# A list scheduler inside the kernel orders the work of every engine: cross attention with a state, then a mixture-of-depths layer

## The chip, the cores and the metric

The kernel runs on one core of a Trainium2 chip. Its engines, TensorE (PE), VectorE (DVE), ScalarE (ACT), GpSimd (POOL) and SyncE (SP), each carry out a queue of instructions in order and wait for each other by semaphores. The metric is the device time of one execution in microseconds; the median of three runs of the kernel before is 334.57 us (334.52 to 334.78).

## The reference

Inputs: x of 8 batches, 8 heads, 512 rows of 64; a state of 32 rows per batch and head; a gate vector of 512; weights w1 (512 x 1024) and w2 (1024 x 512). All is float32, and 128 rows of each batch are chosen.

```python
scores = scale * x @ state.T                 # per batch and head
a = exp(scores - max); a /= sum(a) + 1e-9
xread = a @ state                            # 512 rows
a2 = softmax over x of scale * state @ x.T   # the other direction
sread = a2 @ x                               # 32 rows
x2 = concat([xread, sread], rows), heads side by side   # 8 x 544 x 512
s = x2 @ w_gate                              # one score per row
for b in range(8):
    top = the 128 rows of batch b with the largest s
    out[b] = x2[b]
    out[b, top] += sigmoid(s[top]) * (relu(x2[b, top] @ w1) @ w2)
```

## The kernel before, in words

The work on a batch falls into three parts. The **attention** turns x on TensorE (`turn_x`, L181, copies on ScalarE, L183), multiplies it with the turned state (`scores`, L193), and runs two softmaxes on the same scores: one over the state, for which VectorE transposes blocks of 32 into a tile `e` and back into `eT` (`soft_a` and `soft_b`, L203 to L229), and one over x, on the scores as they lie (`a`, L212). `reads` makes the x read from `eT` (L245, copied by L246 into `xs`) and the state read from the turned `a` (L255, L265, scaled into `xt` by L267). The **choice** multiplies `xs` and `xt` with the gate (`gate_scores`, L291, L295, L298, L299), turns the scores into a row (`score_row`, L306 to L310), compares each with all later ones (`later_wins`, L320), counts the wins on TensorE (L340), makes a one-hot matrix of places (L350) and picks the rows' numbers with a matmul (`gather`, L361); GpSimd then fetches the 128 rows from the output in memory, where `store_base` has put the batch. The **network** (`mlp`) turns the fetched rows (L397), does the first layer (L406, eight groups of columns with a relu on ScalarE, L408) and the second (L415), adds the gated result to the rows (L419) and GpSimd writes them back (L420). It is done for the groups of batches [0], [1], [2, 3], [4, 5], [6, 7].

The order of every engine is that of the code. A loop goes over the batches; at four places of a batch `fill(3.4)` draws pieces of the network from a Python generator that yields an estimate (3.5 us a piece) until 3.4 us are filled. A piece of the first layer is 16 matmuls, one of the second 4. PSUM has two banks with the tag `tr` for all transposes and small products, two banks `h` for the network, and one double bank each for the scores (`s`) and the x read (`o`).

The function that the diff touches is the whole program:

Of the kernel before, what the change touches and what calls it, by code (L numbers as in the profile page):

```python
# [18 lines left out]
def kernel(  # L19
# [38 lines left out]
    N_X, N_XR = 5, 6  # L58
    const = pool("const", 1)
    xin = pool("xin", N_X)  # L60
    work = pool("work", 2)
    xrow = pool("xrow", 2)
    small = pool("small", 4)
    psum = pool("psum", 2, space=bass.MemoryType.PSUM)

    def bank(tag):
        return psum.tile([128, 512], F32, name=f"ps_{tag}", tag=tag)

    def banks(tag):
        return psum.tile([128, 1024], F32, name=f"ps_{tag}", tag=tag, bufs=1)  # L70


    ctx.enter_context(tc.manual_schedule(engines={ENG.PE, ENG.DVE, ENG.Activation, ENG.SP}))
# [3 lines left out]
    xf = {}  # L77

    def load_x(b, pieces=2):
        xf[b] = xin.tile([128, H, NC, D], F32, name="xf")  # L80
        n = H // pieces
        for h in range(0, H, n):
            nc.sync.dma_start(out=xf[b][:, h:h + n], in_=x[b, h:h + n].rearrange("h (p c) d -> p h c d", c=NC))


    st_c = xin.tile([128, B, 2, 2, D], F32, name="st_c", tag="xf")
    st_src = state.rearrange("b (g q) n d -> (q n) b g d", g=2)
    for u in range(2):
        nc.sync.dma_start(out=st_c[:, 0, :, u], in_=st_src[:, 0])
    load_x(0, 4)  # L90
    nc.sync.dma_start(out=st_c[:, 1:B, :, 0], in_=st_src[:, 1:B])

    wg = const.tile([128, Dm], F32, name="wg")
    nc.sync.dma_start(out=wg, in_=bass.AP(tensor=moe_w_gate.tensor, offset=moe_w_gate.offset,
                                          ap=[[0, 128], [1, Dm]]))
    load_x(1)
    load_x(2)
    w1 = const.tile([128, ND, F], F32, name="w1")
    w2 = const.tile([128, NF, Dm], F32, name="w2")
    nc.sync.dma_start(out=w1, in_=moe_w1.rearrange("(j p) f -> p j f", p=128))  # L100
    load_x(3)
    nc.sync.dma_start(out=w2, in_=moe_w2.rearrange("(j p) m -> p j m", p=128))

    ident = const.tile([128, 128], F32, name="ident")
    make_identity(nc, ident)
    z0 = small.tile([128, 1], F32, name="z0")
    nc.vector.memset(z0, 0.0)
    nc.scalar.activation(out=z0, in_=z0, func=AF.Exp)


    st_v = const.tile([128, B, 2, 2 * D], F32, name="st_v")

    def state_V(lo, hi):
# [5 lines left out]
    nc.gpsimd.memset(st_v[:, 0:1], 0.0)  # L119
    state_V(0, 1)  # L120
    nc.gpsimd.tensor_copy(out=st_c[:, 1:B, :, 1], in_=st_c[:, 1:B, :, 0])
    nc.gpsimd.memset(st_v[:, 1:B], 0.0)
    state_V(1, B)

    wg_s = const.tile([128, 2, D], F32, name="wg_s")
    for q in range(4):
        nc.gpsimd.tensor_copy(out=wg_s[Ns * q:Ns * (q + 1)],
                              in_=wg[Ns * q:Ns * (q + 1)].rearrange("p (g m) -> p g m", g=2)[:, :, D * q:D * (q + 1)])


    after = const.tile([128, SP], F32, name="after")
    nc.gpsimd.iota(after, pattern=[[1, SP]], base=0, channel_multiplier=-1, allow_small_or_imprecise_dtypes=True)
    nc.gpsimd.tensor_scalar(after, after, 0.0, None, op0=ALU.is_gt)

    places = const.tile([128, NC + 1, n_slots], F32, name="places")
    nc.gpsimd.iota(places, pattern=[[-128, NC + 1], [1, n_slots]], base=0, channel_multiplier=-1,
                   allow_small_or_imprecise_dtypes=True)
    ones = const.tile([128, 1], BF16, name="ones")
    nc.gpsimd.memset(ones, 1.0)

    same_n = const.tile([128, Ns], F32, name="same_n")

    sc = const.tile([128, B, NC + 1], F32, name="sc")
    nc.gpsimd.memset(sc, 0.0)
    aux = const.tile([128, B, NC + 1, 5], BF16, name="aux")
    num = const.tile([128, 2, B, NC + 1], I32, name="num")
    nc.gpsimd.iota(num[:, 0, :, 0:NC], pattern=[[SP, B], [1, NC]], base=0, channel_multiplier=NC)
    nc.gpsimd.iota(num[:, 0, :, NC], pattern=[[SP, B]], base=S, channel_multiplier=1)  # L150
# [9 lines left out]
    st_T = const.tile([128, B, 2, 128], F32, name="st_T")  # L160

    def state_T(lo, hi):
        for b in range(lo, hi, 2):
            n = min(2, hi - b)
            ps = bank("tr").rearrange("p (b g m) -> p b g m", b=2, g=2)
            for bb in range(n):
                for g in range(2):
                    nc.tensor.transpose(ps[:, bb, g], st_c[:, b + bb, g].rearrange("p u d -> p (u d)"), ident)  # L168
            nc.scalar.activation(out=st_T[:, b:b + n], in_=ps[:, 0:n], func=AF.Copy, scale=scale)  # L169


    xT = {}

    def turn_x(b):

        xT[b] = []
        for h in range(0, H, 2):
            ps = bank("tr").rearrange("p (k r t) -> p k r t", k=2, r=2)
            for k in range(2):
                for r in range(2):  # L180
                    nc.tensor.transpose(ps[:, k, r], xf[b][:, h + k, 2 * r:2 * r + 2].rearrange("p w d -> p (w d)"), ident)  # L181
            t = work.tile([128, 2, 2, 128], F32, name="xT", tag="xT", bufs=6)
            nc.scalar.copy(out=t, in_=ps)  # L183
            xT[b].append(t)

    def scores(b):

        ps = banks("s").rearrange("p (w g t) -> p w g t", w=2, g=2)
        for g in range(2):
            for q in range(4):  # L190
                for w in range(2):
                    half = slice(D * w, D * (w + 1))
                    nc.tensor.matmul(ps[Ns * q:Ns * (q + 1), w, g], st_T[half, b, g, Ns * q:Ns * (q + 1)],  # L193
                                     xT[b][2 * g + q // 2][half, q % 2].rearrange("p r t -> p (r t)"),
                                     start=True, stop=True)
        del xT[b]
        return ps

    def soft_a(ps):

        e = work.tile([128, 32, Ns], F32, name="e")
        flat = e.rearrange("p j n -> p (j n)")
        nc.vector.transpose(out=flat, in_=ps.rearrange("p w g t -> p (w g t)"))  # L203
        nm = small.tile([128, 2], F32, name="nm")
        nc.vector.tensor_reduce(out=nm, in_=ps.rearrange("p w g t -> p g w t"), axis=AX.XY, op=ALU.max, negate=True)  # L205
        mx = small.tile([128, 32], F32, name="mx")
        nc.vector.reduce_max(out=mx, in_=e, axis=AX.X)  # L207
        nc.vector.tensor_tensor(out=e, in0=e, in1=mx.to_broadcast([128, 32, Ns]), op=ALU.subtract)  # L208
        a = work.tile([128, 2, 2, 256], F32, name="a", tag="a", bufs=1)
        ss = small.tile([128, 2], F32, name="ss")  # L210
        for g in range(2):
            nc.scalar.activation(out=a[:, g], in_=ps[:, :, g], func=AF.Exp, bias=nm[:, g:g + 1],  # L212
                                 accum_out=ss[:, g:g + 1])
        nc.scalar.activation(out=flat, in_=flat, func=AF.Exp)
        return e, a, ss

    def soft_b(e, a, ss):

        flat = e.rearrange("p j n -> p (j n)")
        sm = small.tile([128, 32], F32, name="sm")  # L220
        nc.vector.reduce_sum(out=sm, in_=e, axis=AX.X)
        nc.vector.tensor_scalar_add(sm, sm, 1e-9)
        nc.vector.reciprocal(out=sm, in_=sm)
        nc.vector.tensor_tensor(out=e, in0=e, in1=sm.to_broadcast([128, 32, Ns]), op=ALU.mult)
        eT = work.tile([128, 2, 2, 2, 128], F32, name="eT")
        nc.vector.transpose(out=eT.rearrange("p w g r t -> p (w g r t)"), in_=flat)
        rs = small.tile([128, 2], F32, name="rs")
        nc.vector.tensor_scalar_add(rs, ss, 1e-9)  # L228
        nc.vector.reciprocal(out=rs, in_=rs)  # L229
        return eT, a, rs  # L230

    xs, xt = {}, {}

    def reads(b, eT, a, rs):

        xs[b] = xrow.tile([128, NC, Dm], F32, name="xs")
        xt[b] = xrow.tile([128, 2, D], F32, name="xt")

        def x_read(r):
# [232 lines left out]
    for i in range(1, B + 1):  # L472
# [4 lines left out]
        if i < B:  # L477
            ps = scores(i)
# [63 lines left out]
```

## Time and profile before

| | |
|---|---|
| median of three runs | 334.57 us |
| the profiled execution | 335.67 us |
| its span, first to last instruction | 333.9 us |
| mean granted TensorE clock | 0.815 |
| TensorE busy | 239.7 us (72%) |
| VectorE busy | 147.8 us (44%) |
| ScalarE busy | 84.9 us (25%) |

The span is one execution as the hardware profiler saw it. Busy is the time in which an engine had an instruction under way. The granted clock is the share of full speed (2.4 GHz) that TensorE was given; a single stretch is at full or at half speed, or a mean of both.

### The profile page before, as it was taken

How to read it: one execution, taken by the hardware profiler on the slowest of the kernel's cores; microseconds unless marked ns; L12 is line 12 of the kernel's file. 1: busy time of each engine (PE TensorE's matmuls, PEld its weight loads, DVE VectorE, ACT ScalarE, POOL GpSimd, SP SyncE). 2: the span in 40 equal slices, each digit the busy share in tenths (PEclk: the TensorE clock that was granted, in tenths of full speed). 3: DMA queues.
4: the chain of work that ended last, by engine and by line, in shares of the span. 5: the costliest groups of instructions: out<-in, count | busy, mean ns of one | idle time of the engine just before them, and what ended most of it. 6: DMA issues, size and time to landing. Idle time of an engine off the chain costs nothing.

```text
span 333.9 us, 4768 instructions
## 1 busy us (share of the span) xinstructions
PE 239.7 (72%) x1928; PEld 166.1 (50%) x1928; DVE 147.8 (44%) x430; ACT 84.9 (25%) x159; POOL 28.9 (9%) x44
## 2 busy tenths in 40 slices
PE   4308532939992999449597998894949995949993
PEld 3106421738651865237375853453637742428741
DVE  0065639182638182685138537842097315510010
ACT  4027160333313313143115323231131400011100
POOL 4820000100011001100100010011000011010011
PEclk9957855778997898956587979598597976978999
DMA  7995420260054004500300040004000120010000
GB/s 196 315 384 214 171 90 1 84 208 3 0 172 152 2 0 151 174 0 34 133 2 0 0 167 2 32 29 171 0 0 2 69 99 31 1 63 2 0 31 31
DMA packets 17559, 26.86 MB, mean 80 GB/s; under 512 B 5632, under 2 KB 13824, under 8 KB 16512
## 3 DMA queue, kind: packets, MB, share of 16 engines
q1 hardware_dynamic: 16256, 22.35, 19.5%
q0 software_dynamic: 1280, 4.20, 3.9%
q8 instruction: 15, 0.25, 0.3%
q14 instruction: 8, 0.07, 0.1%
HBM read 15.53 MB, written 11.01 MB: 79 GB/s over the span
## 4 chain that ended last, share of the span: by engine, by line
PE 58%; DVE 21%; ACT 7%; DMA 5%; issue 5%; POOL 3%; SPq 1%; POOLq 0%; DVEq 0%; ACTq 0%
PE ps_h L406 19%; PE ps_h L415 17%; PE ps_o L245 6%; DVE scr L291 3%; DMA xr<-out_dram,idx 3%; PE ps_tr L181 3%; DVE e L203 3%; DVE mx L207 3%; DVE nm L205 3%; DVE e L208 3%; PE ps_tr L265 2%; PE ps_s L193 2%; PE ps_tr L361 2%; ACT xs L246 2%; DMA st_c<-in_state_dram 2%
## 5 line engine op out<-in xcount | busy, mean ns | idle before, releaser
L406 PE MATMUL ps_h<-xg,w 128*128 128x256 f32 (+1 forms) x320 | 72.5, 394 | 14.3 <-ACT xg L398 14.3
L406 PEld LDWEIGHTS ps_h<-xg,w 128*128 128x128 f32 x320 | 60.9, 229 | 24.2 <-ACT xg L398 16.0
L415 PE MATMUL ps_h<-w,hT 128*128 128x512 f32 x128 | 68.4, 691 | 0.0
L415 PEld LDWEIGHTS ps_h<-w,hT 128*128 128x128 f32 x128 | 27.2, 220 | 31.9 <-issue 31.6
L181 PE MATMUL ps_tr<-ident,xf 128*128 128x128 f32 x128 | 22.8, 335 | 16.6 <-ACT xT L183 15.9
L181 PEld LDWEIGHTS ps_tr<-ident,xf 128*128 128x128 f32 x128 | 17.9, 170 | 21.4 <-ACT xT L183 18.4
L212 ACT ACTIVATE a<-ps_s,nm 128x512 f32<-128x512 f32 x16 | 10.8, 682 | 61.0 <-DVE nm L205 61.0
L320 DVE SCALAR_TENSOR_TENSOR win<-srow,sc,after 128x544 bf16<-128x544 f32 (+4 forms) x40 | 18.1, 513 | 18.3 <-ACT srow L310 18.3
L367 POOL DMA_INDIRECT xr<-out_dram,idx x8 | 8.0, 994 | 208.6 <-DVE z L373 169.2
L408 ACT ACTIVATE hT<-ps_h 128x512 f32<-128x512 f32 x16 | 9.5, 595 | 63.5 <-PE ps_h L406 63.5
L246 ACT COPY xs<-ps_o 128x1024 f32<-128x1024 f32 x16 | 16.2, 1013 | 33.2 <-PE ps_o L245 33.2
L203 DVE STREAM_TRANSPOSE e<-ps_s 128x1024 f32<-128x1024 f32 x8 | 10.0, 1246 | 33.1 <-PE ps_s L193 31.4
L245 PE MATMUL ps_o<-st_v,eT 64*128 64x128 f32 x256 | 21.6, 317 | 3.5 <-DVE rs L228 2.9
L245 PEld LDWEIGHTS ps_o<-st_v,eT 64*128 64x128 f32 x256 | 18.4, 218 | 8.8 <-DVE rs L228 3.0
L291 DVE SCALAR_TENSOR_TENSOR scr<-xs,wg 128x512 f32<-128x512 f32 x32 | 22.1, 690 | 1.3
L183 ACT COPY xT<-ps_tr 128x512 f32<-128x512 f32 x32 | 17.8, 585 | 7.0 <-PE ps_tr L181 6.7
L267 DVE TENSOR_TENSOR xt<-ps_tr,rs 128x128 f32<-128x128 f32 x8 | 2.3, 292 | 35.8 <-PE ps_tr L265 35.8
L419 DVE SCALAR_TENSOR_TENSOR ot<-ps_h,z,xr 128x512 f32<-128x512 f32 x8 | 6.0, 750 | 26.7 <-PE ps_h L415 26.5
L168 PE MATMUL ps_tr<-ident,st_c 128*128 128x128 f32 x16 | 3.3, 356 | 18.5 <-ACT st_T L169 14.3
L420 POOL DMA_INDIRECT out_dram<-ot,idx x8 | 8.3, 1036 | 86.9 <-DVE ot L419 42.6
L397 PE MATMUL ps_tr<-ident,xr 128*128 128x128 f32 x32 | 7.0, 358 | 11.0 <-DMA xr<-out_dram,idx 11.0
L361 PE MATMUL ps_tr<-aux,oh 128*128 128x5 bf16 (+1 forms) x40 | 7.2, 180 | 10.0 <-DVE oh L350 9.4
(80 smaller groups left out, 238.2 us busy)
## 6 DMA issues: line engine op xcount, KB each, us to landing
out_dram<-xs SPq DMA_DIRECT2D x8, 1024.0 KB, 4.0
xf<-in_x_dram SPq DMA_DIRECT2D x14, 512.0 KB, 6.9
w<-in_moe_w_dram SPq DMA_DIRECT2D x2, 2048.0 KB
xf<-in_x_dram SPq DMA_DIRECT2D x4, 256.0 KB
out_dram<-xt SPq DMA_DIRECT2D x32, 16.0 KB, 3.1
st_c<-in_state_dram SPq DMA_DIRECT2D x1, 448.0 KB
wg<-in_moe_w_gate_dram SPq DMA_DIRECT2D x1, 256.0 KB
st_c<-in_state_dram SPq DMA_DIRECT2D x2, 64.0 KB, 1.9
```

What stands on the lines that cost most here:

```text
L181: nc.tensor.transpose(ps[:, k, r], xf[b][:, h + k, 2 * r:2 * r + 2].rearrange("p w d -> p (w d)"), ident)
L183: nc.scalar.copy(out=t, in_=ps)
L203: nc.vector.transpose(out=flat, in_=ps.rearrange("p w g t -> p (w g t)"))
L205: nc.vector.tensor_reduce(out=nm, in_=ps.rearrange("p w g t -> p g w t"), axis=AX.XY, op=ALU.max, negate=True)
L212: nc.scalar.activation(out=a[:, g], in_=ps[:, :, g], func=AF.Exp, bias=nm[:, g:g + 1], accum_out=ss[:, g:g + 1])
L245: nc.tensor.matmul(po[:, i, w, g], eT[half, w, g, r], st_v[half, b, g], start=True, stop=True)
L246: nc.scalar.copy(out=xs[b][:, 2 * r:2 * r + 2].rearrange("p w (g i m) -> p w g i m", g=2, i=2), in_=po.rearrange("p i w g m -> p w g i m"))
L291: nc.vector.scalar_tensor_tensor(scr, xs[b][:, c], 1.0, wg, op0=ALU.mult, op1=ALU.mult, accum_out=sc[:, b, c:c + 1])
L320: nc.vector.scalar_tensor_tensor(w[0:n], srow[0:n, f:SP], sc[0:n, b, c:c + 1], after[0:n, 0:SP - f], op0=ALU.is_gt, op1=ALU.mult, accum_ou ...
L361: nc.tensor.matmul(pa[0:m, 0:5], oh[0:n, c, lo:hi], aux[0:n, b, c], start=(c == 0), stop=(c == NC))
L406: nc.tensor.matmul(ph[:, f, 0:n], w1[:, j, 128 * (f0 + f):128 * (f0 + f + 1)], xg[:, j], start=(j == 0), stop=(j == ND - 1))
L415: nc.tensor.matmul(py[0:m], hT[:, f, lo:lo + m], w2[:, f], start=(f == 0), stop=(f == NF - 1))
```

## The change

The program no longer issues its instructions where the code stands. It describes pieces: each has an engine, a length in us that was written down, the pieces that it comes after, the buffers that it takes from a ring or uses, and a key. A scheduler, `carry_out`, then issues them: it keeps a clock for each engine, finds for each piece that can go the time at which its engine, its predecessors (0.2 us later if on another engine) and its buffers are free, takes the engine with the earliest such piece, and issues on it the piece of the smallest key among those that can start within 0.25 us of it. Keys are (batch, step) for attention and choice and (100 + group, step) for the network, so the network comes where nothing else can start; its copies and final products come first wherever they are ready. GpSimd's queue is ordered so too.

With it change: the groups of batches of the network, the size of its pieces (4 or 8 matmuls in the first layer, 2 in the second), the buffers of fetched rows (8 instead of 6), and rings of some other small tiles. Behind each indirect DMA GpSimd sets one small tile to zero. The split of the row numbers (`row_numbers`) becomes a piece with a late key. What is computed, and by which instructions, stays the same.

```diff
-    N_X, N_XR = 5, 6
+    N_X, N_XR = 5, 8
...
+    def carry_out():
+        free = {}
+        left = list(pieces)
+        HOP, SOON = 0.2, 0.25
+        while left:
+            ready = []
+            for p in left:
+                if any(q.end is None for q in p.after) or any(buf.ap is None for buf in p.uses):
+                    continue
+                at = max([free.get(p.engine, 0.0)] + [(q.end + HOP if q.engine != p.engine else q.done) for q in p.after])
...
+            t, e = min(((at, p.engine) for at, p in ready), key=lambda r: r[0])
+            at, p = min(((at, p) for at, p in ready if p.engine == e and at <= t + SOON), key=lambda r: r[1].key)
+            for buf in p.takes:
+                buf.ring.take(buf)
+            p.fn()
+            free[e] = p.done = at + p.length
+            p.end = p.done + p.lands
...
+    p_num = add("DVE", 1.0, row_numbers, after=[p_tab], key=(0, 40))
...
+        p = add("DVE", 1.25, turn_in, after=[p_s], takes=[e], uses=[s], key=key(2))
+        p = add("DVE", 1.2, x_max, after=[p], uses=[e], key=key(2))
...
+            p = add("PE", 1.16, read, after=[p_eT, p_pool], takes=[o], uses=[eT], key=key(5))
...
+        return [add("SP", 3.0, x_rows, after=p_xs, uses=[xs], key=(b, 7), lands=1.5),
+                add("SP", 0.4, s_rows, after=[p_xt], key=(b, 7), lands=2.5)]
+    def by_number(b, **kw):
+        touches(b, nc.gpsimd.indirect_dma_start(**kw), True)
+        nc.gpsimd.memset(z1, 0.0)
...
+            for f in range(nf):
+                p = add("PE", 1.86 if nf == 2 else 1.0, lambda f0=f0, f=f, go=first_layer: go(f0, f), after=p_xg + [p_w1],
+                        takes=[] if f else [ph], uses=[xg] + ([ph] if f else []), key=key(1))
...
+            for f0 in range(0, NF, 2):
+                p = add("PE", 1.86, lambda f0=f0, go=second_layer: go(f0), after=p_h + [p_w2], takes=[] if f0 else [py],
+                        uses=[hT] + ([py] if f0 else []), key=key(2))
...
-    groups = [[0], [1], [2, 3], [4, 5], [6, 7]]
+    groups = [[0], [1, 2], [3, 4], [5, 6], [7]]
```

Three places of the new order follow. VectorE's queue at the start held this before (`e` is the tile of the first softmax, `num` and `aux` the row numbers):

```order
L153 TENSOR_REDUCE same_n<-ident 128x32
L154 TENSOR_SCALAR num<-num 128x40
L155 TENSOR_SCALAR num<-num 128x40
L157 CAST aux<-num 128x40 x2
L203 STREAM_TRANSPOSE e<-ps_s 128x1024
L205 TENSOR_REDUCE nm<-ps_s 128x2
```

and holds this now:

```order
L339 STREAM_TRANSPOSE e<-ps_s 128x1024
L343 TENSOR_REDUCE mx<-e 128x32
L346 TENSOR_TENSOR e<-e,mx 128x1024
L367 TENSOR_REDUCE nm<-ps_s 128x2
...
L491 SCALAR_TENSOR_TENSOR scr,part_s<-xt,wg_s 128x128
L485 SCALAR_TENSOR_TENSOR scr,sc<-xs,wg 128x512 x2
L228 TENSOR_REDUCE same_n<-ident 128x32
L229 TENSOR_SCALAR num<-num 128x40
```

The split of the row numbers has moved behind the first softmax and two gate products.

TensorE's queue around the choice of batch 1 and the network of batch 0 held this before (`part_s` is the state rows' gate product, `sc` the scores to be turned, `xr` the fetched rows):

```order
L397 MATMUL ps_tr_599<-ident_99,xr_485 128x128 x4
L406 MATMUL ps_h_606<-xg_598,w1_92 128x128 x16
L181 MATMUL ps_tr_624<-ident_99,xf_95 128x128 x4
L181 MATMUL ps_tr_631<-ident_99,xf_95 128x128 x4
L181 MATMUL ps_tr_638<-ident_99,xf_95 128x128 x4
L181 MATMUL ps_tr_645<-ident_99,xf_95 128x128 x4
L298 MATMUL ps_tr_663<-part_s_660,same_n_131 32x1
L406 MATMUL ps_h_666<-xg_598,w1_92 128x128 x16
L306 MATMUL ps_tr_685<-ident_99,sc_132 128x128 x4
```

and holds this now:

```order
L514 MATMUL ps_tr_613<-ident_76,sc_83 128x128 x4
L498 MATMUL ps_tr_621<-part_s_618,same_n_82 32x1
L276 MATMUL ps_tr_631<-ident_76,xf_72 128x128 x2
L517 MATMUL ps_tr_643<-ident_76,sc_83 128x32
L644 MATMUL ps_tr_646<-ident_76,xr_548 128x128 x4
L661 MATMUL ps_h_659<-xg_652,w1_74 128x128 x4
L302 MATMUL ps_tr_668<-ident_76,xf_641 128x128 x4
L302 MATMUL ps_tr_677<-ident_76,xf_641 128x128 x4
L661 MATMUL ps_h_659<-xg_652,w1_74 128x128 x4
L560 LDWEIGHTS win0_655
```

The score row of batch 1 no longer stands behind two pieces of sixteen matmuls; the first layer comes in fours, and the transposes between (`xf_641`) are those of batch 4.

TensorE's queue ended like this before, from the last pick (`oh` is the one-hot matrix) to the end:

```order
L361 LDWEIGHTS oh
L361 MATMUL ps_tr<-aux,oh 128x5
L397 MATMUL ps_tr<-ident,xr 128x128 x8
L406 MATMUL ps_h<-xg,w_92 128x256 x32
L415 MATMUL ps_h<-w_93,hT 128x512 x16
```

and ends like this now:

```order
L588 LDWEIGHTS oh
L588 MATMUL ps_tr<-aux,oh 128x5
L644 MATMUL ps_tr<-ident,xr 128x128 x8
L661 MATMUL ps_h<-xg,w_74 128x256 x32
L644 MATMUL ps_tr<-ident,xr 128x128 x4
L678 MATMUL ps_h<-w_75,hT 128x512 x16
L661 MATMUL ps_h<-xg,w_74 128x256 x32
L644 MATMUL ps_tr<-ident,xr 128x128 x4
L678 MATMUL ps_h<-w_75,hT 128x512 x16
L661 MATMUL ps_h<-xg,w_74 128x128 x32
L678 MATMUL ps_h<-w_75,hT 128x512 x8
```

Behind the last pick stood two units of the network; now five do (two pairs and a single).

## Rows read from the trace of the kernel before

**Rows 1.** The page's busy times: engine, us, share of the span, instructions.

```profile
PE 239.7 (72%) x1928; PEld 166.1 (50%) x1928; DVE 147.8 (44%) x430; ACT 84.9 (25%) x159; POOL 28.9 (9%) x44
```

**Rows 2.** Waits: who waited, for whom, us in all, times, longest.

```profile
DVE xt L267 <- PE ps_tr L265: 35.8, 8, 6.0
DVE e L203 <- PE ps_s L193: 31.4, 4, 13.2
ACT srow L307 <- PE ps_tr L306: 30.5, 4, 21.7
DVE num L154 <- POOL num L150: 17.0, 1, 17.0
DVE sc L299 <- PE ps_tr L298: 17.0, 8, 7.3
```

**Rows 3.** Stretches: length, busy us of each engine (instructions), clock, DMA share, GB/s.

```profile
35.00:66.00 31.00, 16.19 (x232) 12.31 (x221) 17.31 (x50) 8.79 (x16) 1.18 (x1) 0.61 0.24 84
66.00:101.00 35.00, 27.86 (x267) 20.66 (x266) 18.37 (x53) 9.88 (x19) 1.51 (x2) 0.90 0.32 105
```

**Rows 4.** The chain that ended last, in order: start us, us, what.

```profile
30.86 1.11 PE ps_o L245 x16
32.00 1.02 ACT xs L246
...
47.59 1.07 PE ps_tr L306 x4
48.68 0.59 ACT srow L307
...
58.26 2.01 PE ps_o L245 x16
...
81.20 3.77 PE ps_h L406 x32
84.97 0.44 PE ps_tr L306 x4
...
185.97 3.65 PE ps_h L406 x16
...
299.33 15.54 PE ps_h L406 x64
```

**Rows 5.** Timeline of the start: start us, us, engine, line, operation, idle before.

```profile
8.69 1.38 PE L193 MATMUL ps_s<-xT,st_T 64*32 64x256 f32 x32
...
16.91 1.59 POOL L133 TENSOR_SCALAR after<-after 128x544 f32<-128x544 f32 x1
...
18.91 0.18 DVE L154 TENSOR_SCALAR num<-num 128x40 int32<-128x40 int32 x1 [17.00 <-POOL num L150]
...
19.54 1.24 DVE L203 STREAM_TRANSPOSE e<-ps_s 128x1024 f32<-128x1024 f32 x1
...
35.77 3.42 SPq L286 DMA_DIRECT2D out_dram<-xt  x4
```

**Rows 6.** A stretch of the start in which TensorE had nothing to do.

```profile
16.00:18.00 2.00, 0.00 (x0) 0.00 (x0) 0.00 (x0) 0.00 (x0) 1.93 (x3) 0.50 1.04 394
```

**Rows 7.** Groups by line: shapes, count, busy us, mean ns, idle before.

```profile
L419 DVE SCALAR_TENSOR_TENSOR ot<-ps_h,z,xr 128x512 f32<-128x512 f32 x8 | 6.0, 750 | 26.7 <-PE ps_h L415 26.5
L381 DVE TENSOR_SCALAR z<-z 128x1 f32<-128x1 f32 x8 | 1.2, 144 | 22.0 <-ACT z L380 22.0
```

**Rows 8.** Timeline of the end.

```profile
291.79 1.08 PE L361 MATMUL ps_tr<-aux,oh 128*128 128x5 bf16 x5 [0.72 <-DVE oh L350]
...
297.56 1.09 PE L397 MATMUL ps_tr<-ident,xr 128*128 128x128 f32 x4 [4.11 <-DMA xr<-out_dram,idx]
...
314.71 13.90 PE L415 MATMUL ps_h<-w,hT 128*128 128x512 f32 x32
...
329.67 0.97 POOL L420 DMA_INDIRECT out_dram<-ot,idx  x1 [5.89 <-DVE ot L419]
```

More of the change, by code (lines that the diff above doesn't have):

```diff
@@ L73 @@
[L73 to L86, printed above, removed]
+    work = pool("work", 1)
+    small = pool("small", 6)
+    psum = pool("psum", 1, space=bass.MemoryType.PSUM)
@@ new lines, with __init__, add @@
+    class Piece:
+        def __init__(self, engine, length, fn, after, takes, uses, key, lands):
+            self.engine, self.length, self.fn, self.key, self.lands = engine, length, fn, key, lands
+            self.after, self.takes, self.end = [p for p in after if p], takes, None
+            self.uses = uses
+            self.done = None
+            for buf in list(takes) + list(uses):
+                buf.users.append(self)
+    pieces = []
+    def add(engine, length, fn, after=(), takes=(), uses=(), key=(), lands=0.0):
+        pieces.append(Piece(engine, length, fn, after, takes, uses, key, lands))
+        return pieces[-1]
@@ L131 @@
[L131 to L138, printed above, removed]
@@ new lines, in turn, with keep @@
+                    nc.tensor.transpose(ps[:, bb, g], st_c[:, lo + bb, g].rearrange("p u d -> p (u d)"), ident)
+        def keep():
+            ps = buf.ap.rearrange("p (b g m) -> p b g m", b=2, g=2)
+            nc.scalar.activation(out=st_T[:, lo:hi], in_=ps[:, 0:n], func=AF.Copy, scale=scale)
+        t = add("PE", 0.3 * n, turn, after=[p_st0] if lo == 0 else [p_st, p_pool], takes=[buf], uses=[stb], key=key)
+        k = add("ACT", 0.3 * n, keep, after=[t], uses=[buf], key=key)
+        for b in range(lo, hi):
+            p_sT[b] = k
@@ L508, with turn, keep @@
-    fill(1e9)
+        xg, hT = Buf(R_XG), Buf(R_HT)
+        p_xg = []
+        for u, lo in zip(units, at):
+            m, pt = u["m"], Buf(P_TR)
+            def turn(u=u, m=m, pt=pt):
+                v = pt.ap.rearrange("p (j s) -> p j s", j=ND)
+                for j in range(ND):
+                    nc.tensor.transpose(v[:, j, 0:m], u["xr"].ap[0:m, 128 * j:128 * (j + 1)], ident[0:m, 0:m])
+            def keep(m=m, pt=pt, lo=lo):
+                nc.scalar.copy(out=xg.ap[:, :, lo:lo + m], in_=pt.ap.rearrange("p (j s) -> p j s", j=ND)[:, :, 0:m])
+            p = add("PE", 0.55, turn, after=[u["got"]], takes=[pt], uses=[u["xr"]], key=key(0))
+            p_xg.append(add("ACT", 0.59, keep, after=[p], takes=[] if p_xg else [xg], uses=[pt] + ([xg] if p_xg else []),
+                            key=NOW))
@@ new lines @@
+    groups = [[0], [1, 2], [3, 4], [5, 6], [7]]
+    chosen, number = [], 0
+    state_T(0, 1, (0, 0))
+    for b in range(B):
+        if b == 1:
+            for lo in range(1, B, 2):
+                state_T(lo, min(lo + 2, B), (lo, -1))
+        if b >= 4:
+            load_x(b, (b, -2))
+        got = attention(b)
+        if not cap:
+            continue
+        chosen += choice(b, *got)
+        while len(chosen) >= 2 and n_tiles > 1:
+            layers(chosen[:2], number)
+            chosen, number = chosen[2:], number + 1
+        if chosen and ((n_tiles == 1 and any(b == g[-1] for g in groups)) or b == B - 1):
+            layers(chosen, number)
+            chosen, number = [], number + 1
```

706 lines of the change are left out of this document (385 added, 321 removed).

## The prediction, made before the changed kernel had run

> **What bounds the kernel now.** I read the page's busy shares first. TensorE (PE) is busy for 72% of the span and VectorE (DVE) for 147.8 us, 44% [rows 1]: no engine is full, so the time lies in engines that wait for each other. The list of waits says how [rows 2]. VectorE stood 35.8 us for the state read, 31.4 us for the scores and 17.0 us for one column of the gate score, all of them TensorE's work; ScalarE stood 30.5 us for the transposed score row, which VectorE needs next. TensorE is not slow at those: they are short, but stand in its queue behind long pieces of the two-layer network. The stretches by batch show both sides [rows 3]. From 35 to 66 us, with no network work, one batch takes 31.0 us, VectorE is busy for 17.31 of them and TensorE for 16.19. From 66 to 101 us, with one unit of the network, it takes 35.0 us and VectorE is busy for 18.37. So a batch costs VectorE about 18 us and takes 31 to 35, because its softmax, its choice of rows and the network follow each other. The kernel is bound by the order of its queues.
>
> **The start.** The scores of batch 0 end on TensorE at 8.69 + 1.38 = 10.07 us, but VectorE starts on them at 19.54 us: ahead of them in its queue stands the split of the row numbers, which waits for the last GpSimd table until 18.91 us [rows 2, 5]. In the new order the softmax of batch 0 stands first, and the split comes after two gate products, when its table is long there. What this removes is 9.4 us. What is next late is the scores themselves, at 10.1 us; the transposes of batch 1 behind them depend on loads that I can't see land, but VectorE has the first softmax to do meanwhile. The softmax of batch 0 now runs beside GpSimd's copies and tables, which in the kernel before had finished or left VectorE idle. The longest of them in the rows is 1.59 us [rows 5]. The cost of that is bounded by zero and by both two-input softmax instructions waiting for one such instruction, 3.2 us; I take zero, since most of VectorE's rows of the softmax read one operand, and keep 3.2 for the range. The Trainium skill, "SBUF — State Buffer", section "Who interferes with whom", says that a VectorE instruction with two SBUF inputs and a GpSimd instruction that reads SBUF lock each other out for a whole instruction. No row of the kernel before has the two side by side at the start; by that rule the sum below would be up to 3.2 us longer.
>
> **From the first softmax to the last choice.** VectorE's instructions stay the same: of 147.8 us, five of the eight final products (750 ns each) and six small gate instructions (about 144 ns each) come after the last choice, which leaves 147.8 - 3.75 - 0.9 - 0.1 = 143 us [rows 1, 7]. To these come waits. Without any, the last choice would be made at 10.1 + 143 = 153 us. If each batch waited as in the stretch from 35 to 66 us, 31.0 - 17.31 = 13.7 us, it would be 8 x 13.7 = 110 us more [rows 3]. Between them I count the handoffs of a batch that leave VectorE and come back: the x read and its copy (2.01 + 1.02 us at the lower clock), the score row and its copy (1.07 + 0.59), the scores (1.38) and the pick (1.08), together 7.2 us [rows 4, 5, 8]. In the new order VectorE has instructions of another batch between the two ends of most of these: after the output turn of one batch come the wins and the one-hot of the one before. Batch 0 has nothing to put there, the last batches end with three choices in a row, and elsewhere TensorE reaches the handoff late. I take half, 3.6 us a batch, and 0.9 us for a network piece in the way, a quarter of sixteen instructions at 3.65 us [rows 4]: 4.5 x 8 = 36 us. The last choice then comes at 10.1 + 143 + 36 = 189 us, where it now ends at 291.79 + 1.08 = 292.9 us [rows 8].
>
> TensorE can keep this pace if its clock stays up. The trace shows 0.61 of full clock in the stretch where it was busy for half of the time, 0.90 where it was busy for 80% [rows 3], and 0.50 after some us with nothing to do [rows 6]. The same sixteen x-read matmuls took 1.11 us and 2.01 us, the four transposes of the score row 0.44 and 1.07 [rows 4]. The handoffs above are counted at the lower level for this reason. Each network unit costs 2 x 3.77 us in its first layer alone, or 2 x 3.65 as half of a pair, and 13.90 / 2 = 6.95 in its second [rows 4, 8]. By the new order three units (batch 0, and the pair 1 and 2) are done before the last choice: 7.5 + 7.0 + 14.6 + 13.9 = 43 us of TensorE that VectorE does not wait for in the sum.
>
> **After the last choice.** Five units remain, and nothing stands between them but TensorE's own rows, since their rows were fetched before (only the last unit's fetch is recent, and it is used 60 us later). Transposes and first copy: 1.09 us and 299.33 - 297.56 = 1.8 us. The first pair: 15.54 + 13.90. The second pair at the faster rate: 4 x 3.65 = 14.6, + 13.90. The last unit: 2 x 3.77 = 7.5, + 6.95. Two transposes between: 2 x 1.09 = 2.2; one wait for the hidden layer's copy, about 1 us (the nearest copy of that size took 0.59). The end of the kernel after the last matmul is as now: 333.9 - (314.71 + 13.90) = 5.3 us [rows 4, 8]. Sum: 1.1 + 1.8 + 15.5 + 13.9 + 14.6 + 13.9 + 7.5 + 7.0 + 2.2 + 1 + 5.3 = 83.8 us. Now it is 333.9 - 292.9 = 41.0 us with two units and a wait for the last fetch. Three units more in a tail that is dense cost less than they do among the batches, where they hold up VectorE.
>
> **Smaller edits.** Eight buffers of gathered rows instead of six, small tiles in rings of their own and GpSimd's order written out change no instruction. One memset behind each of 16 indirect DMAs stands on an engine that is busy for 9% of the span [rows 1]; behind it wait only the next fetches, which are not late: nothing. On SyncE's queue the load of x for batch 4 now stands behind the four small stores of batch 1, which take 3.42 us to issue there [rows 5], where the plan counts 0.4. TensorE's transposes of it stand ahead of batch 1's count of wins, so this costs between zero and 3.4 us; it is one of the late handoffs that I have in the 36 us.
>
> **Sum.** 10.1 + 143 + 36 + 83.8 = 272.9 us of span. The profiled execution took 335.67 us for a span of 333.9, 1.8 more, and stands 1.1 above the median of 334.57, so the time as the runs give it is the span plus 0.7: 273.6, and I say 273 us.
>
> **Rivals.** *VectorE hardly waits.* If the planned order holds almost as written, waits of about 20 us are left (2.5 a batch), and the time is 257 us. For it: the lengths written into the plan are near the rows. Against it: they are those of full clock.
>
> *TensorE sets the pace of the attention.* Eight batches at the 16.19 us of the stretch at 0.61 clock are 130 us, with the 43 us of network 173 us, more than VectorE's 143; if TensorE is kept busy for 80% of the time, as in its denser stretch [rows 3], the last choice comes at 10.1 + 216 = 226 us and the time is 311; with half of that loss, 290. For it: between the second layer of batch 0 and the first pair of the network, for about three batches, TensorE has attention alone, the kind of work that ran at 0.61. Against it: TensorE's busy share rises, and with it, in rows 3, the clock. The Trainium skill, "TensorE: Matmul & The Clock Gate", section "What's actually happening", says that the array is throttled by default and that activity lifts it; the rows agree (0.50 idle, 0.90 busy). By that rule thin stretches cost double, and dense tails nothing.
>
> *Slower than before.* The interleaving does not take hold: an in-order queue that meets one late producer passes the delay to the other engines, and each batch keeps the 13.7 us of waits. Then 10.1 + 143 + 110 + 83.8 + 0.7 = 348 us. It decides from 97 us of waits, 12.1 a batch, that is, when nearly nothing of the old waiting goes. For it: the new tail is 43 us longer than the old one, all of which has to be won back earlier. Against it: most of the old waits are for rows behind long network pieces, and those are now cut into pieces of four or eight.
>
> **How the numbers follow.** The forecast, waits of 25 to 51 us, 262 to 288 us, gets 0.60; hardly any waits, below 262, 0.15; TensorE's pace, 288 to 315, 0.20; slower than before 0.035; between these and no change 0.015. The range from 257 to 297 us leaves out about 0.07 below and 0.12 above. About 0.2% is what a measurement of this kernel can tell from no change: faster 0.955, the same 0.01, slower 0.035.
>
> **What would show it.** The first 128x1024 transpose on VectorE at 10 us, the last pick near 189 us and from there a stretch of some 78 us in which TensorE is busy throughout at nearly full clock. VectorE's busy time stays at 147 to 149 us. Between 10 and 189 us VectorE is busy for about 80%. The waits for the state read and the score row shrink to a few us each. If the last pick comes after 205 us and TensorE is busy there for over 85%, at a granted clock of 0.7 or less, TensorE sets the pace. If the tail takes more than 90 us, the five units were not ready. If VectorE's two-input instructions are longer than 1.3 us between 10 and 19 us, GpSimd is in their way.

## The result, and the profile after

The changed kernel takes 250.41 us (median of four runs, 248.68 to 251.3), the kernel before on the same chip 334.54 us. The ratio is 0.748, with a 95% interval of 0.7439 to 0.7521. The forecast was 273 us with a range of 257 to 297: the direction and most of the gain were right, and the time lies 23 us below the forecast and 7 us below its range.

First, the same rows of the page as [rows 1]: busy time, share of the span and instructions of each engine.

```profile
PE 209.8 (85%) x1928; PEld 150.7 (61%) x1928; DVE 145.8 (59%) x430; ACT 86.0 (35%) x159; POOL 32.4 (13%) x60
```

The instructions of TensorE (PE) and VectorE (DVE) are as many as before, 1928 and 430. VectorE's busy time fell by 2.0 us only, TensorE's from 239.7 to 209.8. So TensorE's part of the span went from 239.7 busy + 94.2 idle = 333.9 us to 209.8 busy + 37.1 idle = 246.9 us: 57.1 us of the gain of 87.0 are gaps that closed, and for 29.9 us the same matmuls kept TensorE busy for less time, at a higher granted clock (mean 0.92 of full speed, where it was 0.815). That all of the 29.9 us are the clock is not shown.

Next, the stretches of the changed kernel, with the columns of [rows 3]. The first row is the whole way from the first softmax to the end of the last pick, the second a thin stretch inside it, the last the tail.

```profile
10.37:170.10 159.73, 132.50 (x1591) 98.67 (x1592) 140.36 (x416) 73.60 (x137) 20.16 (x34) 0.88 0.42 143
...
95.00:127.00 32.00, 22.11 (x324) 17.24 (x325) 29.02 (x97) 13.88 (x24) 2.68 (x4) 0.79 0.21 79
...
170.10:246.90 76.80, 71.37 (x289) 48.13 (x288) 5.35 (x14) 8.21 (x15) 7.65 (x14) 0.99 0.07 24
```

VectorE is busy for 140.36 of 159.73 us, 88%. It waits for 19.4 us, 2.4 a batch, where it waited for 13.7 in the undisturbed batch of [rows 3]. The waits of VectorE between 10 and 170 us, with the columns of [rows 2], say what is left of them:

```profile
DVE e L339 <- PE ps_s L325: 9.5, 1, 9.5
DVE xt L439 <- PE ps_tr L434: 3.7, 4, 2.5
DVE off L566 <- PE ps_tr L560: 3.5, 2, 2.2
DVE pick L592 <- PE ps_tr L588: 2.2, 3, 0.9
DVE sm L353 <- ACT e L349: 1.7, 1, 1.7
DVE scr L485 <- ACT xs L405: 1.3, 2, 0.7
DVE win L533 <- ACT srow L523: 0.7, 2, 0.6
```

The 9.5 us are the start, before 10.37 us. Without them the rows above add up to 13.1 us; the rest of the 19.4 are smaller waits and short gaps between VectorE's own instructions. The wait for the state read fell from 35.8 to 3.7 us, that for the scores from 31.4 to the start alone, and the count of wins waits for the score row for 0.7 us.

The timeline of the start (start us, us, engine, line, operation, idle before) shows the softmax where [rows 5] has an idle VectorE:

```profile
10.37 1.25 DVE L339 STREAM_TRANSPOSE e<-ps_s 128x1024 f32<-128x1024 f32 x1 [9.51 <-PE ps_s L325]
...
12.91 1.40 DVE L346 TENSOR_TENSOR e<-e,mx 128x1024 f32<-128x1024 f32 x1
...
17.18 1.22 DVE L353 TENSOR_REDUCE sm<-e 128x32 f32<-128x1024 f32 x1 [1.74 <-ACT e L349]
```

And the timeline of TensorE's end, beside [rows 8]:

```profile
169.75 0.35 PE L588 MATMUL ps_tr<-aux,oh 128*128 128x5 bf16 x5
170.03 1.45 PE L644 MATMUL ps_tr<-ident,xr 128*128 128x128 f32 x8
171.36 14.08 PE L661 MATMUL ps_h<-xg,w 128*128 128x256 f32 x64
...
185.72 13.90 PE L678 MATMUL ps_h<-w,hT 128*128 128x512 f32 x32
199.45 13.98 PE L661 MATMUL ps_h<-xg,w 128*128 128x256 f32 x64
...
213.70 13.90 PE L678 MATMUL ps_h<-w,hT 128*128 128x512 f32 x32
227.44 7.31 PE L661 MATMUL ps_h<-xg,w 128*128 128x128 f32 x64
234.58 7.03 PE L678 MATMUL ps_h<-w,hT 128*128 128x512 f32 x16
```

Five units after the last pick, as forecast, back to back from 170.03 to 241.6 us, and 5.3 us more to the end of the kernel.

### The profile page after: what moved, and what is told of

The parts are those of the page before. It is cut to its first block, busy times and chain, and to the rows that moved or that the text cites. A ratio compares the mean times of both kernels' runs of the same rounds, so it can differ in the third digit from the quotient of the medians.

```text
span 246.9 us, 4781 instructions
## 1 busy us (share of the span) xinstructions
PE 209.8 (85%) x1928; PEld 150.7 (61%) x1928; DVE 145.8 (59%) x430; ACT 86.0 (35%) x159; POOL 32.4 (13%) x60
## 4 chain that ended last, share of the span: by engine, by line
PE 29%; DVE 28%; issue 28%; ACT 4%; DMA 4%; POOL 3%; SPq 2%; POOLq 1%; DVEq 0%; ACTq 0%
PE ps_o L402 7%; PE ps_h L678 6%; PE ps_h L661 4%; DVE scr L485 4%; DMA xf<-in_x_dram 4%; PE ps_tr L302 3%; DVE win L533 3%; DVE eT L361 3%; DVE e L358 2%; DVE sm L353 2%; DVE e L346 2%; DVE nm L367 2%; PE ps_tr L434 2%; PE ps_tr L418 2%; POOL out_dram L473 2%
## 5 line engine op out<-in xcount | busy, mean ns | idle before, releaser
L661 PE MATMUL ps_h<-xg,w 128*128 128x256 f32 (+1 forms) x320 | 59.5, 345 | 0.7 <-ACT xg L647 0.7
L678 PE MATMUL ps_h<-w,hT 128*128 128x512 f32 x128 | 58.0, 598 | 0.0
L661 PEld LDWEIGHTS ps_h<-xg,w 128*128 128x128 f32 x320 | 52.3, 196 | 7.3 <-issue 1.4
L678 PEld LDWEIGHTS ps_h<-w,hT 128*128 128x128 f32 x128 | 23.3, 190 | 24.6 <-issue 24.3
L302 PE MATMUL ps_tr<-ident,xf 128*128 128x128 f32 x128 | 23.8, 344 | 5.6 <-DMA xf<-in_x_dram 4.5
L325 PE MATMUL ps_s<-xT,st_T 64*32 64x256 f32 x256 | 10.8, 447 | 9.6 <-ACT a L371 9.6
L418 PE MATMUL ps_tr<-ident,a 128*128 128x128 f32 x64 | 11.0, 312 | 2.1 <-ACT xT L305 2.1
L325 PEld LDWEIGHTS ps_s<-xT,st_T 64*32 64x32 f32 x256 | 4.4, 120 | 13.7 <-ACT a L371 10.9
L421 ACT COPY aT<-ps_tr 128x512 f32<-128x512 f32 x16 | 9.1, 589 | 7.5 <-PE ps_tr L418 7.5
L349 ACT ACTIVATE e<-e 128x1024 f32<-128x1024 f32 x8 | 8.5, 1061 | 9.1 <-DVE e L346 9.1
```

Source lines behind the costliest of these rows:

```text
L302: nc.tensor.transpose(v[:, k, r], xf[b].ap[:, 2 * pair + k, 2 * r:2 * r + 2].rearrange("p w d -> p (w d)"), ident)
L325: nc.tensor.matmul(view_s()[Ns * q:Ns * (q + 1), w, g], st_T[half, b, g, Ns * q:Ns * (q + 1)], xT[2 * g + q // 2].ap[half, q % 2].rearrang ...
L418: nc.tensor.transpose(v[:, c], a.ap[:, g, c % 2, 128 * (c // 2):128 * (c // 2 + 1)], ident)
L661: nc.tensor.matmul(v[:, f, 0:n], w1[:, j, 128 * (f0 + f):128 * (f0 + f + 1)], xg.ap[:, j, 0:n], start=(j == 0), stop=(j == ND - 1))
L678: nc.tensor.matmul(py.ap[0:m], hT.ap[:, f, lo:lo + m], w2[:, f], start=(f == 0), stop=(f == NF - 1))
```

## The experiments

Two theories were to be told apart. *Order covers the handoffs*: they are as long as the prediction counted, but VectorE nearly always has another batch's work meanwhile. *Clock shortens the handoffs*: with the network between, TensorE stays at a high clock and answers sooner. Later the question became what a wait of VectorE costs at all. The table gives for each kernel the time (of those marked with * the median of four runs, else one run), the span, TensorE's busy and idle time in it, and the starts of the first softmax and of the last pick counted from the start of the span, all in us. The kernel before took 331.1 to 336.0 beside them on the same chips. A difference of 2 us between two single runs tells nothing.

| kernel | time | span | TensorE busy + idle | first softmax | last pick |
|---|---|---|---|---|---|
| before* | 334.54 | 333.9 | 239.7 + 94.2 | 19.5 | 292.7 |
| after* | 250.41 | 246.9 | 209.8 + 37.1 | 10.4 | 169.9 |
| no mixing of batches | 260.77 | 259.0 | 217.9 + 41.1 | 10.5 | 224.2 |
| network last | 295.0 | 293.2 | 225.6 + 67.6 | 11.4 | 171.6 |
| network last, TensorE kept busy | 312.27 | 310.5 | 288.7 + 21.8 | 11.3 | 189.1 |
| large network pieces | 250.92 | 249.1 | 212.6 + 36.5 | 10.2 | 204.9 |
| before, network last | 348.44 | 346.7 | 234.1 + 112.6 | 19.8 | 219.2 |
| before, first softmax early | 326.07 | 324.3 | 237.5 + 86.8 | 10.2 | 283.1 |
| after, first softmax late | 252.32 | 250.5 | 210.1 + 40.4 | 21.0 | 173.6 |
| equal lengths in the plan | 265.93 | 264.1 | 215.5 + 48.6 | 16.3 | 227.6 |
| fetched rows turned at once* | 232.68 | 232.2 | 205.4 + 26.8 | 11.3 | 184.5 |
| the same, other pairs* | 234.8 | 232.4 | 203.5 + 28.9 | 11.0 | 196.5 |
| network first* | 270.86 | 269.2 | 216.2 + 53.0 | 10.3 | 241.5 |

**No mixing of batches.** The softmax of a batch begins on VectorE only after the pick of the batch before, and TensorE turns the x of a batch only after the pick of the batch two before it.

```
- p = add("PE", 0.53, turn, after=[...] + last_turn[-1:], ...)
+ p = add("PE", 0.53, turn, after=[...] + last_turn[-1:] + picks[-2:-1], ...)
...
- p = add("DVE", 1.25, turn_in, after=[p_s], ...)
+ p = add("DVE", 1.25, turn_in, after=[p_s] + picks[-1:], ...)
```

> The softmax of a batch may only begin on VectorE when the row numbers of the batch before are picked (and x of the batch after next is turned only then); the scheduler orders the rest as it likes. Theory 'order covers' (VectorE's waits are small because rows of another batch stand between the two ends of a handoff): waits of 10 to 14 us a batch come back, last pick at 10.4 + 141 + 8 x 10 to 14 = 231 to 263 us; the network has more room beside it, three pairs and a single instead of three units, so a tail of about 25 us with one or two units: about 265 to 290 us. Rival 'clock' (waits are small because TensorE runs at full clock): waits only to about 6 us a batch, last pick near 200 us, 225 to 240 us in all.

The mixing covers a large part of the handoffs: without it the last pick comes 54 us later. VectorE is busy for 145.5 of the 213.9 us up to it and so waits for 68 us, 8.5 a batch, where it waits for 2.4 in the changed kernel:

```profile
10.50:224.40 213.90, 183.12 (x1763) 133.57 (x1764) 145.51 (x419) 79.80 (x148) 23.76 (x39) 0.87 0.31 110
```

The result lies between the two theories, the last pick (224 us) and the time (261) both: the order theory wanted 231 to 263 and 265 to 290 us, the clock theory about 200 and 225 to 240. The kernel is only 10 us slower than after, since TensorE did the network in VectorE's waits, and was busy for 183 us of that stretch instead of 132.5.

**Network last.** In the new order all network pieces come after the last pick.

```
- p = add("PE", 0.55, turn, after=[u["got"]], ...)
+ p = add("PE", 0.55, turn, after=[u["got"]] + last_index, ...)
```

> All eight units of the network come after the last pick, so TensorE has attention and choice alone until then. Theory 'clock' (the waits that I counted at TensorE's lower level shrank because the network's pieces keep its clock up): clock of 0.6 to 0.7 in the attention, waits of VectorE back to 30 to 36 us, last pick at 181 to 188 us. Theory 'order covers': last pick at 165 to 172 us whatever the clock. After it 42 + 77 us of network: 300 to 309 us by the clock, 284 to 293 us by the order.

The stretch from the first softmax to the last pick:

```profile
11.40:171.80 160.40, 103.00 (x1399) 76.20 (x1400) 138.86 (x413) 68.93 (x127) 16.35 (x29) 0.72 0.39 138
```

The granted clock is 0.72 there instead of 0.88, and one of its sixteen x reads shows the long form of [rows 4]; the groups of the x reads (`ps_o`, sixteen reads) and the scores (`ps_s`, eight) follow, first of this run, then of after (count | busy us, mean ns | idle before):

```profile
158.48 2.08 PE L402 MATMUL ps_o<-st_v,eT 64*128 64x128 f32 x16 [2.09 <-DVE z L613]
...
L402 PE MATMUL ps_o<-st_v,eT 64*128 64x128 f32 x256 | 25.0, 352 | 5.3 <-DVE z L613 2.1
L325 PE MATMUL ps_s<-xT,st_T 64*32 64x256 f32 x256 | 15.7, 631 | 20.2 <-ACT a L371 20.2
...
L402 PE MATMUL ps_o<-st_v,eT 64*128 64x128 f32 x256 | 22.2, 323 | 4.6 <-DVE rs L376 4.2
L325 PE MATMUL ps_s<-xT,st_T 64*32 64x256 f32 x256 | 10.8, 447 | 9.6 <-ACT a L371 9.6
```

So an x read takes 25.0 / 16 = 1.56 us on average against 1.39 in after, and the scores of a batch 15.7 / 8 = 1.96 us against 1.35. Yet VectorE waits for 160.4 - 138.9 = 21.5 us against 19.4: handoffs that are longer at the lower clock are covered nearly as well. The clock theory wanted the last pick at 181 to 188 us; it came at 171.6, as the order theory had it, and the clock theory fell. (The time, 295.0, is 2 us above the range of the order theory.) In sum the network between the batches costs VectorE nothing in the changed kernel: it makes the handoffs shorter, and what its pieces cost by standing in the way is no more than that. The run doesn't part the two.

**Network last, TensorE kept busy.** The same with twelve pieces of four matmuls a batch added, whose result nobody reads, at the lowest priority.

```
+ add("PE", 0.5, warm, after=[p_s, p_pool], takes=[idle], key=(99, k))
```

> As the run with the network last, but with twelve pieces a batch of four matmuls (128 columns) whose result nobody reads, placed where nothing else can start: only TensorE's busy time and clock change. Theory 'clock': clock of 0.85 or more, last pick 8 to 15 us earlier than with the network last. Theory 'order covers': last pick within 3 us of the run with the network last (or later, where a piece is in the way).

The stretch from 11 to 189 us, up to its last pick:

```profile
11.00:189.00 178.00, 166.04 (x2173) 149.57 (x2165) 140.34 (x413) 68.35 (x127) 16.71 (x29) 0.96 0.36 125
```

The clock is 0.96, and the last pick comes 17 us later than without these pieces: VectorE waits for 178.0 - 140.3 = 37.7 us. Filling TensorE to 93% of the stretch takes more from VectorE than the clock gives; what the clock alone would give, this run doesn't show.

**Large network pieces.** Pieces of 16 to 32 matmuls instead of four or eight, in the new order.

```
- for f0 in range(0, NF, 2):
-     p = add("PE", 1.86, lambda f0=f0, go=second_layer: go(f0), ...)
+ for f0 in range(0, NF, 8):
+     p = add("PE", 7.44, lambda f0=f0, go=second_layer: go(f0), ...)
```

> The changed kernel with network pieces as large as they can be: a whole bank of the first layer (16 or 8 matmuls, 3.7 us) and the whole second layer of a unit (8 matmuls of 512 columns, 7 us) instead of 4 or 8 and 2. If fine pieces are what keeps VectorE fed, its waits rise by about 3 us for each of the nine large pieces before the last pick: last pick at 180 to 195 us, 257 to 272 us in all. If only the keys matter (network where nothing else can start), 249 to 255 us.

The large pieces do stand in VectorE's way, the last pick is 35 us later; but more of the network is done by then, the tail is 44 us instead of 77, and the time is the same. The last pick came later than either expectation had it (180 to 195 us at most), the time as the second had it. The size of the pieces is not what the gain rests on.

**Before, network last.** The kernel before, its network held back until the end, with nine buffers of fetched rows.

```
+ if us < 1e6:
+     return
```

> The kernel before, in its own order, with the network drawn only at the end (nine buffers of fetched rows instead of six); to be held against the new order with the network last, whose last pick came at 171.8 us. If the order of attention and choice alone is what feeds VectorE, the old one takes 25 to 31 us a batch: last pick at 220 to 265 us, 340 to 385 us in all. If the old waits were only network pieces in the way, the last pick comes at 180 to 195 us, 300 to 315 us in all.

With no network in either, the old order takes 219.2 - 19.8 = 199.4 us from the first softmax to the last pick, the new one 160.2: 39 us are due to the new order of attention and choice, 8.4 us to the start, and the rest of the 53.5 between the two spans to the tail (127.5 against 121.6). (The new rings of small tiles are part of the new order here; they were not taken back by themselves.) VectorE's waits in this stretch, of the kernel before with its network and of this run:

```profile
19.50:293.00 273.50, 201.88 (x1768) 141.25 (x1769) 143.94 (x414) 76.92 (x144) 13.32 (x13) 0.79 0.21 75
...
20.00:219.00 199.00, 107.94 (x1388) 84.72 (x1388) 136.15 (x387) 67.77 (x120) 7.39 (x7) 0.67 0.27 94
```

VectorE waited for 129.6 us before, and for 62.9 us without the network: in the old order the network accounts for about half of the waits, and the order of attention and choice for most of the others, since the new order without network leaves 21.5.

**Before, first softmax early.** The split of the row numbers stands behind the first reads, in the old order.

```
- row_numbers()
...
+ row_numbers()
```

> The kernel before with one move: the split of the row numbers behind the first softmax and reads on VectorE. By the prediction's start term the whole program begins 9.2 us earlier and, since the chain of waits before runs through VectorE's first transpose, 323 to 326 us. If loads or TensorE's first batches take its place, 330 us or more.

8.8 us less than the kernel before beside it (334.86), where the prediction had 9.4 for the start.

**After, first softmax late.** The reverse, in the new order.

```
- p = add("DVE", 1.25, turn_in, after=[p_s], ...)
+ p = add("DVE", 1.25, turn_in, after=[p_s] + ([p_num] if b == 0 else []), ...)
```

> The changed kernel with the first softmax made to come after the split of the row numbers; the scheduler orders the rest around it. VectorE's first transpose at 19 to 21 us instead of 10.4. If the time is set by VectorE until the last pick, all of it comes out at the end: last pick at 178 to 182 us, 257 to 260 us. If TensorE's fill takes part of it back (it idles later in the attention anyway), 250 to 255 us.

The softmax begins 10.6 us later, the last pick comes 3.7 us later, the span is 3.6 us longer. The same 10 us cost 8.8 in the old order and at most 4 in the new.

**Equal lengths in the plan.** Every piece of TensorE, VectorE and ScalarE counts as 1.0 us when the order is made.

```
- pieces.append(Piece(engine, length, ...))
+ pieces.append(Piece(engine, 1.0 if engine in ("PE", "DVE", "ACT") else length, ...))
```

> The scheduler with 1.0 us for every piece on TensorE, VectorE and ScalarE instead of the written lengths; keys, rings and pieces as they are. If the written lengths matter, queues are ordered for times that don't come, and waits of VectorE grow by 10 us or more: 260 us or more. If keys and readiness do the work, 245 to 256 us.

15 us slower than after: the written lengths are worth something, but the interleaving without them still gains 69 us.

**Fetched rows turned at once.** One key of the changed kernel: the transposes of fetched rows stand ahead of all attention pieces instead of behind them.

```
- p = add("PE", 0.55, turn, after=[u["got"]], takes=[pt], uses=[u["xr"]], key=key(0))
+ p = add("PE", 0.55, turn, after=[u["got"]], takes=[pt], uses=[u["xr"]], key=NOW)
```

> The changed kernel with one key changed: the transposes of fetched rows go first wherever they are ready, instead of waiting for a free transpose bank behind all attention. By the new order the pair 3 and 4 is then also done before the last pick, and three units are left instead of five: 49 us of tail instead of 77. TensorE stood idle for 27 us between 10 and 170 us, so at most that much can be won: last pick at 175 to 195 us, 225 to 242 us in all. If TensorE's pieces hold up VectorE as in the run with warming matmuls, last pick at 200 us and 248 us or more.

A better kernel than both: 232.68 us (231.88 to 234.0), 0.6978 of before (0.6934 to 0.7022). In the changed kernel the rows of the first pair were there early, the second of its picks is made at 88 us, its fetch is issued at 89.8, and no fetch took more than 6.1 us to land. But the transposes of them all stood behind the attention of two more batches, from 122.98 us on, and the pair's first layer began at 127.20. The last piece of network work before it ended at 88.33 + 1.98 us:

```profile
88.33 1.98 PE L678 MATMUL ps_h<-w,hT 128*128 128x512 f32 x4
...
122.98 0.63 PE L644 MATMUL ps_tr<-ident,xr 128*128 128x128 f32 x4
...
127.20 7.07 PE L661 MATMUL ps_h<-xg,w 128*128 128x256 f32 x32
```

That is the thin stretch above, 22.11 of 32 us at a clock of 0.79. With the new key it is filled; the transposes, the first layer and the stretch:

```profile
89.08 0.66 PE L644 MATMUL ps_tr<-ident,xr 128*128 128x128 f32 x4 [0.24 <-ACT xT L305]
...
91.34 1.89 PE L661 MATMUL ps_h<-xg,w 128*128 128x256 f32 x8
```

```profile
95.00:127.00 32.00, 30.45 (x350) 22.76 (x348) 25.68 (x78) 14.40 (x27) 2.15 (x2) 1.00 0.21 78
```

TensorE is busy for 8.3 us more of it, and its idle time in the whole span fell by 10.3. VectorE pays, 25.68 us of work instead of 29.02, and the last pick comes 15 us later; the kernel is 18 us faster.

**The same, other pairs.** Batches 0 and 1 are a pair, 2 and 3, 4 and 5; 6 and 7 are alone.

```
- groups = [[0], [1, 2], [3, 4], [5, 6], [7]]
+ groups = [[0, 1], [2, 3], [4, 5], [6], [7]]
```

> As the run before, with the network's groups [0, 1], [2, 3], [4, 5], [6], [7], so that pairs come early and two singles last. One unit and a bit are left after the last pick, but the first network work starts a batch later: 224 to 242 us; within 4 us of the run before, either way.

234.8 us (234.14 to 236.49): the last pick is 12 us later again, the time nearly the same. Which batches are paired hardly matters here.

**Network first.** All network pieces of the changed kernel stand ahead of all attention pieces.

```
- return (100 + number, n)
+ return (-1, 100 * number + n)
```

> The changed kernel with the network's keys below all others, so that a network piece goes first wherever it is ready. One unit is left after the last pick, a tail of about 21 us. If TensorE's total work sets the time, idle falls to about 20 us and the time is 228 to 240 us; if holding up VectorE matters as in the kernel before, last pick after 235 us and 256 us or more.

270.86 us (270.2 to 271.76), 20 slower than after. Network pieces now hold the x reads up: VectorE's wait for their copies is 24.9 us, where it is 1.3 in after. The picks come later and with them the fetches, and in the end TensorE itself waits for fetched rows, the longest of its waits here and none in after (how often it waited stands behind the sum):

```profile
DVE scr L485 <- ACT xs L405: 24.9, 4, 16.2
...
PE ps_tr L644 <- DMA xr<-out_dram,idx: 15.2, 4, 5.8
```

## Why the prediction missed

**The start: right.** First softmax at 10.37 us (forecast 10.1). The worth of 9.4 us was right in the old order (8.8) and would have been wrong in the new one (at most 4): the order takes most of a late start back. Of the bound of 3.2 us for GpSimd in the way, one instruction shows 0.2 us (last section). The load of x for batch 4 was late as feared: TensorE waits 1.48 us for it, and VectorE 2.21 us for the count of wins behind it (rows below), inside the bound of 0 to 3.4.

**Waits of VectorE: the step that failed.** The term of 36 us, half of the handoffs and 0.9 us a batch for a network piece in the way, measured 19.4. With the network last the waits are 21.5 us, so the network between the batches adds nothing in sum, where I had 7.2 us for it. And of the counted 7.2 us of handoffs a batch 21.5 / 8 = 2.7 us are left uncovered there, not 3.6. Whether that is more cover or shorter handoffs is not parted: the scores were longer in that run than I had counted (1.96 against 1.38 us), the x reads shorter (1.56 against 2.01). Pieces do stand in the way in places. The longest wait for a count of wins, 2.21 us, lies behind the late transposes of batch 4 and a piece of the first layer:

```profile
56.15 1.97 PE L302 MATMUL ps_tr<-ident,xf 128*128 128x128 f32 x8 [1.48 <-DMA xf<-in_x_dram]
57.91 1.92 PE L661 MATMUL ps_h<-xg,w 128*128 128x128 f32 x8
59.62 0.75 PE L560 MATMUL ps_tr<-ones,win 128*128 128x1 bf16 x15
...
60.41 0.16 DVE L566 TENSOR_TENSOR off<-over,ps_tr 128x4 f32<-128x4 f32 x1 [2.21 <-PE ps_tr L560]
```

The rival "VectorE hardly waits", 20 us and 257 us in all, was this case, and its chance of 0.15 was too low. Its objection, that the plan's lengths are those of full clock, carried little weight: at a clock of 0.72 the waits were 21.5 us, 2 more than at 0.88. VectorE's own work in this stretch was 140.4 us instead of 143. Together 19.3 us of the 26.0 by which the sum was too long in the span (272.9 against 246.9).

**The tail: right in kind, 7.0 us too long.** 76.8 us instead of 83.8, with five units as forecast. I had taken the first pair from the trace of before, where TensorE had stood idle ahead of it: 15.54 us, here 14.08 [rows 4]. TensorE comes to the last pick from network work, and the first pair's rows were turned within 1.45 us of it, without the 2.9 us for transposes and a copy. The wait of 1 us between the layers isn't there: the transposes of the next unit fill it, and these take 0.60 us each, not 1.09. The end after the last matmul is 5.3 us as forecast.

**What no step had.** The sum of the prediction adds VectorE's path up to the last pick and a fixed tail behind it. By that sum 35 us more on the way (large pieces) or 54 (no mixing) make the kernel so much longer. They made it 0 and 10 us longer, since the network then moves from the tail into VectorE's waits; and the fastest version has a later last pick than after. So the two terms are not independent, and where the miss of 19.3 us lies is accounting; that less waiting alone caused it is not shown. The reading that orders the table is TensorE's idle time. In the new order, with the network free to move, the spans of 232.2, 232.4, 246.9, 249.1, 250.5, 259.0, 264.1 and 269.2 us have 26.8, 28.9, 37.1, 36.5, 40.4, 41.1, 48.6 and 53.0 us of it, while the last picks are at 184, 196, 170, 205, 174, 224, 228 and 241 us: the three slowest kernels have the three latest, but the two earliest belong to neither of the two fastest. (Busy and idle make the span by definition; that the idle part carries most of the differences, 26.2 of the 37.0 us between the first and the last, is what the runs show.) By this the "slower" rival had its turning point too early: without mixing VectorE waits for 68 us, 49 more than in after, and the kernel is 10 us slower.

**TensorE sets the pace: wrong, but with one true observation.** Up to the last pick TensorE was busy for 132.5 of 159.7 us at 0.88, and VectorE for 140.4. From 130 us on, after the pair's first layer had begun, TensorE had hardly a gap:

```profile
130.00:150.00 20.00, 19.68 (x209) 15.38 (x207) 19.19 (x36) 10.59 (x21) 0.00 (x0) 1.00 0.13 54
150.00:170.10 20.10, 20.10 (x207) 11.90 (x196) 16.40 (x85) 4.75 (x12) 3.25 (x6) 1.00 0.31 100
```

VectorE waits for 4.5 of these 40.1 us, so this cost the last pick little; but TensorE stays like this up to 241.6 us, and how much work it still has sets the end. The thin stretch that spoke for this rival, attention alone between the first unit's second layer and the first pair, is there: no network for 37 us, from 90.3 to 127.2, and a clock of 0.79. It costs nothing by making VectorE wait; it costs in the tail, where the network is done that was not done in it. The Trainium skill, "TensorE: Matmul & The Clock Gate", section "What's actually happening", has activity lift the clock; the rows agree (0.72 with the network last, 0.96 with the unread pieces added), and the same two runs show that a lift bought with added pieces lost 17 us up to the last pick. What the lift by itself is worth there is not shown.

## What to carry to other kernels

When one engine has a long, patient job and another a chain of short handoffs, don't add up the chain and a tail: count the idle time of the engine that holds the patient work, and look for the stretch where that work was there but not started. Short steps that make such work available (a transpose of fetched rows) go first, the long work itself last: the first is worth 18 us here, the reverse of the second costs 20. Whether waits are covered is tested by taking the other work out, not by taking half.

## What was unexpected of the hardware

VectorE's subtraction with two full inputs took 1.40 us beside GpSimd's copies, where the same instruction has a median of 1.22 over eight batches, and GpSimd's four copies took 4.73 us where they took 3.84 in the kernel before. The whole of that is in the last of the four, which starts while the subtraction (12.91 to 14.31 us) is under way and takes 1.83 us instead of 0.93. With the early softmax in the old order the subtraction took 1.56, and with the fetched rows turned at once 1.74. The rows of the changed kernel, then of these two:

```profile
10.37 4.73 POOL L199 COPY st_v<-xf 32x896 f32<-32x896 f32 x4
13.27 1.83 POOL L199 COPY st_v<-xf 32x896 f32<-32x896 f32 x1
```

```profile
13.68 1.56 DVE L208 TENSOR_TENSOR e<-e,mx 128x1024 f32<-128x1024 f32 x1
...
17.77 1.59 POOL L133 TENSOR_SCALAR after<-after 128x544 f32<-128x544 f32 x1
...
18.22 1.27 DVE L224 TENSOR_TENSOR e<-e,sm 128x1024 f32<-128x1024 f32 x1
```

```profile
13.53 0.93 POOL L199 COPY st_v<-xf 32x896 f32<-32x896 f32 x1
...
13.80 1.74 DVE L346 TENSOR_TENSOR e<-e,mx 128x1024 f32<-128x1024 f32 x1
```

The Trainium skill, "SBUF — State Buffer", section "Who interferes with whom", has a VectorE instruction with two SBUF inputs and a GpSimd instruction that reads SBUF lock each other out for a whole instruction. For the copies the traces agree: the later of the two is longer by nearly what was left of the earlier one. In the changed kernel the last copy starts 1.04 us before the subtraction ends and takes 0.90 us longer; in the last run above the subtraction starts 0.66 us before a copy ends and takes 0.52 us longer. So the price is not a whole instruction but the rest of one: 0.2 to 0.5 us on VectorE, 0.9 on GpSimd. For GpSimd's TENSOR_SCALAR in the second run they don't agree: VectorE's multiplication with two inputs starts beside it at 18.22 us and takes 1.27 us, the TENSOR_SCALAR 1.59 as in the kernel before [rows 5].

The second surprise is how much of the gain came without a shorter program: 29.9 us of TensorE's 87.0 are the same 1928 matmuls in less busy time, at a mean clock of 0.92 instead of 0.815, with the gaps between them closed.
